# Attention and a low-rank mixer on one core: q, k and v loaded into 112 partitions in place of 128

## The chip, the core and the metric

The kernel runs on one core of a Trainium2 chip. The metric is the device time of one execution in microseconds (us), here the median of three runs. The five engines are TensorE (PE in the profile; PEld is its weight load), VectorE (DVE), ScalarE (ACT), GpSimd (POOL) and SyncE (SP), which only issues transfers. Sixteen DMA engines carry the transfers that SP, ACT and POOL issue.

## The reference

For each of 8 batches and 12 heads, with sequence S = 448 and head size D = 64, queries and keys are normalised by their root mean square and a gain, attention is a plain softmax, and the heads of a batch are laid side by side (768 columns). A low-rank mixing over the sequence (rank 32) is added, and a two-layer network with 3072 hidden columns follows, with a residual.

```
q_n, k_n = rmsnorm(q, g_q), rmsnorm(k, g_k)
attn = softmax(q_n @ k_n.T / sqrt(64))
x = heads side by side of (attn @ v)            # (8, 448, 768)
u = x + (x.T @ U @ V).T
out = u + relu(u @ w_ch1) @ w_ch2
```

All inputs and the output are float32.

## The kernel before, in words

A sequence of 448 rows is held as 112 partitions by NJ = 4 rows: partition p holds rows 4p to 4p+3 of a head, 4 x 64 floats, 1 KB that lie together in memory. SP = 112 is that number of partitions (a name in the code, not the engine), P = 128 is the whole of SBUF's partitions. Since a head is 112 such pieces and heads follow each other, pieces 112 to 127 counted from a head's start are the first sixteen pieces of the next head.

The work on heads goes by groups t of four heads (24 groups; `load` and `load_v`, L199 and L204), and by pairs p of two heads (48 pairs, two to a group). `heads` (L188) builds the source pattern of a load: rows, heads, 256 floats. `load_pair` (L195) loads one pair's q or k, 128 or 112 rows of two heads; the first pair is loaded head by head, q by SP and k by ACT (L856 to L859). `load_v` loads v of a group, four heads in one transfer. Buffers lie in turns in three fixed places for q and k (`qkL`, and part of `hT`) and in a few places for v (`vt`, slots of `comb`, part of `hT`); the profile names the transfers by these places.

What is done with a pair: `squares` (L218) on ACT or POOL, `reduce` (L232) on DVE, `rsqrt` (L236) on ACT, `scale` (L241) on DVE or, from pair 12, POOL; then a transposition on PE (pairs 0 to 11) or by a DMA transpose from SP (`dma_transposes`, L277), the scores (L296), the exponentials on ACT (L304), the products with v (L311) and the normalisation on DVE (L326, L335). `cast_v` (L213) on POOL turns v to bf16. All of these read rows 0 to 111 of what was loaded.

The order is written by hand. The first batch follows a list of words, HEAD (L720): `sq`, `R`, `q`, `S` are the four steps above, `T`/`Tq`/`Tk`/`Tl` transposes, `Eq`/`Ek`/`El` their copies out of PSUM, `SC` and `X` scores and exponentials, `V` and `N` products and normalisation, `F` filler matmuls on PE, `G` and `GC` the gains and their copy on ACT, `cast` v's cast, `w` a load of weights by POOL, `late` small preparations on POOL, `MT`/`t`/`MU`/`u` the mixing, `B` the first matmuls of the network. Each engine takes its instructions in this order. ISSUE (L853) hangs the loads of groups 3 and 4 onto three of the words. All loads of groups 0 to 2, U and V stand ahead of it on SP (L856 to L868).

After the head, the network's steps (`mlp_first` L440, `mlp_single` L471, `mlp_pair` L522) fill PE, and the attention and mixing of the later batches are woven between them by weights (`weave`, L686). Loads of group t+3 and v of group t+2 are issued in `attention` (L658 to L662), groups 6 and 7 after a `touch` (L208, one memset on DVE, so that the loads have one thing to wait for). The weights w1 and w2 are loaded by POOL (L177, L181) with a cast to bf16, in six transfers each.

Before the change, `heads` gives 128 rows unless the load reaches the last head of the last batch, where 128 rows would run past the input: there it gives 112. Those are the second pair's q and k of group 23, and its v.

Of the kernel before, what the change touches and what calls it, by code (L numbers as in the profile page):

```python
# [18 lines left out]
def kernel(  # L19
# [14 lines left out]
    B, H, S, D = q.shape  # L34
# [5 lines left out]
    P = 128  # L40
    NJ = 4
    SP = S // NJ
# [144 lines left out]

    def heads(x, h, n):  # L188

        rows = P if h + n < B * H else SP  # L190
        src = x.rearrange("b h s d -> (b h) s d")[h:h + n].rearrange("h (p j) d -> p h (j d)", j=NJ)
        (ps, _), (hs, _), (ls, ln) = src.ap
        return rows, bass.AP(src.tensor, src.offset, [[ps, rows], [hs, n], [ls, ln]])

    def load_pair(eng, t, s, a, hs=slice(0, 2)):  # L195
        rows, src = heads((q, k)[s], HG * t + 2 * a + hs.start, hs.stop - hs.start)
        eng.dma_start(qk_of[t][0:rows, a, s, hs], src)
# [6 lines left out]
    def load_v(t):  # L204
        rows, src = heads(v, HG * t, HG)
        nc.sync.dma_start(v_of[t][0:rows], src)
# [746 lines left out]
```

## Time and profile before

| | us |
|---|---|
| median of 3 runs (566.09 to 568.92) | 568.36 |
| the profiled execution | 566.27 |
| its span, first to last instruction | 564.5 |
| TensorE busy / VectorE / ScalarE / GpSimd | 552.0 / 339.7 / 303.8 / 179.3 |

The core moved 72.39 MB in 108284 packets, 56.78 MB of it read from memory. The page gives, for each engine, the busy time, its share of the span and the number of instructions; then the span in 40 equal slices (14.1 us each) with the busy share of each in tenths; then the chain of work that ended last, by engine. The order of work gives start and duration of an instruction, and in brackets the idle time of its engine just ahead of it with what ended that. A line on transfers gives destination and source, the issuing queue, the number, the size of one, and the median time from issue to landing.

### The profile page before, as it was taken

The page shows a single profiled execution, that of the slowest core. Times are in us where ns is not written, and L with a number is a line of the kernel's source. Part 1 is how long each engine was busy: PE and PEld are TensorE (multiplying, and loading weights), DVE is VectorE, ACT ScalarE, POOL GpSimd, SP SyncE. Part 2 cuts the span into 40 slices and gives each one's busy share as a digit, 9 for nine tenths or more (in the row PEclk, how much of TensorE's full clock was granted, in tenths as well). Part 3 has the DMA queues.
Part 4 walks back from the last instruction along what each step waited for, and adds up shares of the span by engine and source line. Part 5 has one row for each costly group of instructions (what it writes and reads, how often), then busy time and mean ns, then how long its engine had stood idle before and what let it go on. Part 6 is the DMA issues. An engine that isn't in the chain of part 4 may idle for free.

```text
span 564.5 us, 13202 instructions
## 1 busy us (share of the span) xinstructions
PE 552.0 (98%) x5469; PEld 388.2 (69%) x5469; DVE 339.7 (60%) x766; ACT 303.8 (54%) x515; POOL 179.3 (32%) x175
## 2 busy tenths in 40 slices
PE   7999999999999999999999999999999999999996
PEld 3665665767768677576785785776867768677774
DVE  5967858487665655656665577465565644643332
ACT  7966640779347663488448781765716745112020
POOL 5966016444051340432404430434104320010202
PEclk9999999999999999999999999999999999999999
DMA  8999996946455561365357563634615101030102
GB/s 275 283 243 239 204 253 174 206 130 168 129 96 150 144 155 48 76 187 142 87 143 160 130 176 85 152 94 143 168 29 125 30 17 59 15 99 1 57 1 57
DMA packets 108284, 72.39 MB, mean 128 GB/s; under 512 B 56656, under 2 KB 104768, under 8 KB 108224
## 3 DMA queue, kind: packets, MB, share of 16 engines
q1 hardware_dynamic: 96704, 61.70, 41.9%
q0 software_dynamic: 11008, 9.44, 10.3%
q8 instruction: 43, 0.70, 0.5%
q10 hardware_dynamic: 512, 0.41, 0.2%
q14 instruction: 17, 0.14, 0.1%
HBM read 56.78 MB, written 11.01 MB: 120 GB/s over the span
## 4 chain that ended last, share of the span: by engine, by line
PE 89%; ACT 4%; DVE 2%; DMA 2%; issue 1%; SPq 0%; POOLq 0%
PE ph L529 32%; PE po L512 29%; PE o L311 7%; PE po L467 5%; PE sc L296 4%; PE ph L449 3%; PE sh L296 3%; ACT E L304 2%; PE px L388 1%; ACT hT L421 1%; DMA hT<-in_moe_V_dram 1%; DMA qk<-in_q_dram 1%; PE bank L311 1%; PE sc L710 1%; PE ph L477 1%
## 5 line engine op out<-in xcount | busy, mean ns | idle before, releaser
L529 PE MATMUL ph<-ur,w1b 128*128 128x256 bf16 x1728 | 202.7, 273 | 0.0
L529 PEld LDWEIGHTS <-w1b 128*128 128x128 bf16 x1728 | 164.0, 98 | 29.1 <-issue 9.1
L512 PEld LDWEIGHTS <-hT 128*128 128x128 bf16 x1032 | 96.5, 98 | 65.0 <-issue 7.9
L421 ACT ACTIVATE hT<-ph 128x512 bf16<-128x512 f32 (+1 forms) x112 | 65.5, 587 | 116.1 <-PE ph L529 108.6
L304 ACT ACTIVATE E<-sc 112x896 bf16<-112x896 f32 x138 | 123.1, 918 | 2.3 <-PE sc L296 2.3
L248 POOL TENSOR_TENSOR qkn<-qk,rms 112x512 bf16<-112x512 f32 x72 | 80.4, 1138 | 111.2 <-ACT rms L239 86.5
L512 PE MATMUL po<-w2b,hT 128*128 128x384 bf16 (+1 forms) x588 | 103.6, 323 | 0.2 <-ACT hT L421 0.2
L304 ACT ACTIVATE E<-sh 112x448 bf16<-112x448 f32 x108 | 52.9, 543 | 78.6 <-PE sh L296 78.6
L520 DVE TENSOR_TENSOR hT<-hT 128x512 bf16<-128x512 bf16 x144 | 68.4, 492 | 21.3 <-ACT hT L421 19.0
L512 PE MATMUL po<-comb,hT 128*128 128x384 bf16 (+1 forms) x444 | 78.3, 322 | 0.0
L569 POOL TENSOR_TENSOR osb<-osb,xr 128x384 f32<-128x384 f32 x12 | 12.9, 1072 | 189.1 <-DVE osb L568 168.1
L423 DVE TENSOR_SCALAR hT<-ph 128x512 bf16<-128x512 f32 (+1 forms) x58 | 38.7, 667 | 55.6 <-PE ph L529 52.7
L311 PEld LDWEIGHTS <-E 112*128 112x128 bf16 x1536 | 61.1, 98 | 9.0 <-issue 1.9
L311 PE MATMUL o<-va,E 112*128 112x65 bf16 x1344 | 57.0, 194 | 0.2
L326 DVE RECIPROCAL rec<-o 128x4 f32<-128x4 f32 x84 | 15.1, 180 | 50.1 <-PE o L311 50.0
L296 PE MATMUL sc<-qkT 64*128 64x448 bf16 x268 | 39.7, 351 | 1.8 <-ACT E L304 1.1
L233 DVE TENSOR_REDUCE sums<-sq 112x16 f32<-112x1024 f32 x32 | 38.7, 1209 | 3.9 <-ACT sq L228 3.8
L467 PE MATMUL po<-w2b,hT 128*128 128x384 bf16 x192 | 34.7, 326 | 0.1
L228 ACT ACTIVATE sq<-qk 112x1024 f32<-112x1024 f32 x32 | 33.8, 1057 | 0.0
L335 DVE TENSOR_TENSOR xr<-o,rec 128x192 bf16<-128x192 f32 (+1 forms) x108 | 31.6, 311 | 2.9
L581 POOL TENSOR_TENSOR osb<-osb,part 128x768 f32<-128x768 f32 x12 | 21.8, 1814 | 35.7 <-DVE part L579 35.7
L390 DVE TENSOR_TENSOR xr<-px,xr 128x384 bf16<-128x384 f32 x56 | 29.5, 550 | 5.9 <-PE px L386 3.2
(120 smaller groups left out, 444.3 us busy)
## 6 DMA issues: line engine op xcount, KB each, us to landing
qk<-in_q_dram SPq DMA_DIRECT2D x44, 256.0 KB, 4.2
qk<-in_k_dram SPq DMA_DIRECT2D x44, 256.0 KB, 4.7
vt<-in_v_dram SPq DMA_DIRECT2D x17, 512.0 KB, 5.8
w1b<-in_moe_w_ch_dram POOLq DMA_DIRECT2D x6, 768.0 KB, 21.0
w2b<-in_moe_w_ch_dram POOLq DMA_DIRECT2D x6, 768.0 KB, 34.2
out_dram<-osb SPq DMA_DIRECT2D x8, 336.0 KB, 3.0
comb<-in_v_dram SPq DMA_DIRECT2D x5, 512.0 KB, 9.0
out_dram<-osb SPq DMA_DIRECT2D x7, 288.0 KB, 2.9
```

Of the source, the lines that this page charges most:

```text
L228: nc.scalar.activation(dst, src, AF.Square)
L233: nc.vector.tensor_reduce(rs_of(p, of=sums).rearrange("p (s h j) -> p s h j", s=2, h=2)[:, :, hs], sqs[p].rearrange("p (s h j d) -> p s h ...
L248: (nc.gpsimd if p >= 12 else nc.vector).tensor_tensor(out[:, g], x[:, g], rs[:, g].to_broadcast([SP, g.stop - g.start, NJ, D]), OP.mult)
L296: nc.tensor.matmul(sc[hh][0:n, 0:S], flat[pp, c:c + n], blocks(p)[pp, :, 0], start=True, stop=True)
L304: nc.scalar.activation(dst, src, AF.Exp, scale=float(D) ** 0.5)
L311: nc.tensor.matmul(o[:, i, :], E[:, hh, c:c + P], va[:, hl, kc, :], start=(kc == 0), stop=(kc == NJ - 1))
L421: nc.scalar.activation(out, ph, AF.Relu)
L423: nc.vector.tensor_relu(out, ph)
L467: nc.tensor.matmul(po, left(hc), w2b[:, half, hc, :], start=(hc == 0), stop=(hc == KH - 1))
L512: nc.tensor.matmul(bank, left[:, k, :], right[:, k, cols], start=start and k == 0, stop=k == KH // 2 - 1, skip_group_check=not start)
L520: pending.append(lambda: fn(*args))
L529: nc.tensor.matmul(out, w1b[:, dc, hc * P:(hc + 1) * P], u[:, dc, :], start=(dc == 0), stop=(dc == KD - 1))
```

## The change

`heads` takes 112 rows always, not only at the end of the input. Nothing else differs: the same transfers are issued at the same places, each with 112 pieces of 1 KB for each head in place of 128.

```diff
     def heads(x, h, n):

-        rows = P if h + n < B * H else SP
+        rows = SP
         src = x.rearrange("b h s d -> (b h) s d")[h:h + n].rearrange("h (p j) d -> p h (j d)", j=NJ)
         (ps, _), (hs, _), (ls, ln) = src.ap
         return rows, bass.AP(src.tensor, src.offset, [[ps, rows], [hs, n], [ls, ln]])
```

## The prediction

> **What bounds the kernel now.** I read the page from the top, then its chain, then the waits and the order of work in the first 36 us, and last the transfers with their times to landing.
>
> ```profile
> span 564.5 us, 13202 instructions
> PE 552.0 (98%) x5469; PEld 388.2 (69%) x5469; DVE 339.7 (60%) x766; ACT 303.8 (54%) x515; POOL 179.3 (32%) x175
> PE   7999999999999999999999999999999999999996
> PEclk9999999999999999999999999999999999999999
> DMA  8999996946455561365357563634615101030102
> PE 89%; ACT 4%; DVE 2%; DMA 2%; issue 1%; SPq 0%; POOLq 0%
> ```
>
> TensorE is busy 552.0 of 564.5 us, at a granted clock that stays at its top, and 89% of the chain is its own work. The loads that the change touches are 2% of the chain at most. The DMA row is full only at the start. So the change can act in two ways: in the first slice of PE (a 7), which waits for the first loads, and through weights that share the 16 DMA engines with the loads until about 86 us.
>
> The windows of the first 15 us show what PE loses there: 3.68, 3.08 and 4.40 us busy of 5.00 each, so 3.8 us idle, 1.3 of it ahead of the first matmul; part of the busy time is warm-up. The order of work shows what the loads have to do with it (start, duration, then the idle time ahead and who ended it):
>
> ```profile
> 6.91 1.06 ACT L228 ACTIVATE comb<-qk 112x1024 f32<-112x1024 f32 x1 [0.68 <-DMA qk<-in_k_dram]
> ...
> 8.00 1.22 DVE L233 TENSOR_REDUCE sums<-comb 112x16 f32<-112x1024 f32 x1 [0.99 <-ACT gcol L838]
> 8.06 0.81 PE L700 MATMUL sc<-xr 128*128 128x512 bf16 x3 [1.07 <-ACT gcol L838]
> ...
> 8.53 1.06 ACT L228 ACTIVATE w2b<-qk 112x1024 f32<-112x1024 f32 x1 [0.52 <-DMA qk<-in_k_dram]
> ...
> 9.95 1.90 POOL L230 TENSOR_TENSOR w2b<-qk 112x1024 f32<-112x1024 f32 x1 [2.43 <-DMA qk<-in_k_dram]
> ```
>
> Pair 1's squares (6.91) wait for their k. The copy GC is queued behind them on ACT (7.87); the reduction R1 (8.00) and PE's fillers (8.06) wait for GC. From 8.00 on DVE is full: the windows give it 4.96, 4.93, 4.90 and 4.90 us of 5.00 from 10 to 30 us, and from 25 us PE is full too. So R1's start passes through to the end, by DVE first and by PE's queue after. That is the change's one lever on the path.
>
> **The change part by part.** (1) Bytes. Section 6 of the page lists 49 loads of q, 49 of k and 24 of v, 122 in all; three (two of 224 KB, one of 448 KB) have 112 rows already. The other 119 shrink by an eighth: 92 of 256 KB by 32, four of 128 KB by 16, 23 of 512 KB by 64, which is 4480 KB: 4.59 of 72.39 MB, and 4480 of 108284 packets, each of them 1 KB. No instruction, issue or wait is added or removed: every reader reads rows 0 to 111 only, and rows past them are read by nobody.
>
> (2) Issue. SP spent 0.42 and 0.45 us on the two 112-row loads at 399.67 and 400.14 us, and 0.42 to 0.47 on 128-row ones beside them. Cost nothing; no queue is passed.
>
> (3) Time of one transfer. The trace has three of the new form, and neighbours of the old:
>
> ```profile
> vt<-in_v_dram SPq DMA_DIRECT2D x1, 512.0 KB, 6.1
> qk<-in_q_dram SPq DMA_DIRECT2D x1, 256.0 KB, 3.2
> qk<-in_k_dram SPq DMA_DIRECT2D x1, 256.0 KB, 3.6
> qk<-in_q_dram SPq DMA_DIRECT2D x1, 224.0 KB, 5.4
> qk<-in_k_dram SPq DMA_DIRECT2D x1, 224.0 KB, 5.4
> ```
>
> These are the five loads of the last group at 398.5 us, issue to landing. In fifteen earlier groups the third and fourth load, with 128 rows, took 3.3 to 5.4 and 3.5 to 6.7 us, medians 4.2 and 4.8. So two of the new form, with an eighth fewer bytes, landed 1.2 and 0.6 us later than the median of the old. From landing to landing, second to fourth, that is 2.82 us against a median of 2.04 (1.23 to 4.78): 0.39 us more for each load. The lone v of 448 KB reads better:
>
> ```profile
> GB/s 389 307 184 102 102 189 191 205 174 90 41 118 268 260 135 145 61 48 96 273 307 369 389 389 355 273 143 61 27 0 0 0 0 0 0 0 0 0 0 0
> vt<-in_v_dram SPq DMA_DIRECT2D x1, 448.0 KB, 3.9
> ```
>
> This is the window 434 to 440 us in slices of 0.15 us: once it runs it moves 389 GB/s, the rate that 128-row loads reach (374 to 386 in the head at 2 to 3.4 us). From 3.2 us for a first 256 KB and 389 GB/s for the rest, 448 KB in the old form would take 3.7 and 512 KB 3.9 (an estimate). It took 3.9.
>
> So the bounds are: an eighth off each transfer's moving time, or 0.39 us more for each load. I take a value near nothing with a small gain, because the lone load is the one whose rate can be read without a neighbour, and the two late ones lie inside the old form's spread.
>
> [...]
>
> (4) The head. After the four 128 KB loads (the last lands at 4.12 us) two 256 KB loads land until 6.84 us, pair 1's k last: 2.72 us. An eighth of that is 0.34 us, and the gate cannot give more than ACT's 0.68 us of waiting. Behind it sq2 (8.53) and POOL's squares (9.95) wait for loads too; they would land up to 0.5 and 0.7 us earlier by the same share, so they follow and set no new gate. What is late next is POOL's own work ahead of ACT's squares (Sk0 and Sl0, 6.31 to 7.51). Forecast: 0 to 0.34 us less, taken as 0.2.
>
> (5) The weights. w1's six chunks land at 27.6, 33.9, 40.2, 46.4, 52.7 and 57.5 us (issue plus time to landing). PE runs hidden chunks of 128 columns in 1.53 us each (38.3 to 69.0 us, twenty of them), so from the second on they are needed at 38.3, 44.5, 50.6, 56.8 and 62.9: 4.1 us of cover at least. w2's first lands at 61.4, needed at 69.0. Earlier landings here buy nothing, since no PE wait of this stretch is put down to a transfer of weights; later ones cost only beyond 4.1 us.
>
> (6) The steady part. No ACT square after 9 us waits for a load. The tightest covers are pair 16 (k lands 106.3, squares at 107.46) and pair 38 (325.74, 326.65): 1.1 and 0.9 us. Earlier landings change nothing; landings 1.2 us later would cost 0.1 and 0.3 us on ACT.
>
> Sum: the profiled execution took 566.27 us, 1.77 around its span of 564.5. 566.27 - 0.2 = 566.1. That execution was 2.09 us below the median of the runs shown, 568.36; with the same step the forecast is 568.2.
>
> **Rivals.** (A) The forecast: a landing moves by under 0.35 us, the head by 0 to 0.34: 568.0 to 568.4. For it: the lone load's 389 GB/s and its unchanged 3.9 us. Against: the full DMA row at the start, where an eighth could count for more.
> (B) Bytes count in full, and the gate yields all of its 0.68 us: 567.7. For it: the landings of the head come one behind another, at 311 to 330 GB/s. Against: the first 256 KB loads land 0.9 us apart, though 16 engines at 389 GB/s would need 0.67, so bytes are not all of it.
> (C) Slower: 112 rows make each transfer 0.39 us longer. It decides as soon as the second 256 KB load is late: pair 1's k by 0.8 us, pair 3's (six loads on) by 2.3. POOL's squares then end at 14.2 in place of 11.85, and R3, now at 12.01, starts at 14.2: the head loses 2.2 us. The two tight places add 0.4 at most, and w1, with eight q and k loads and two v loads of twice the size beside it, would be late by 0.39 x 12 = 4.7 us, 0.6 beyond its cover. Together 0.8 to 3.2 us: 569.2 to 571.6, taken as 570.6. For it: 5.4 us twice. Against: the old form's spread.
> (D) The change doesn't reach the bytes (fewer engines take a load, or packets of another size). The three loads of that form moved in 1 KB packets, with completions from 16 engines, so I give it nothing of its own.
>
> **How the numbers follow.** A 0.62, B 0.14, C 0.24. The predicted time is A's, 568.2. Runs of before spread over 566.09 to 568.92, so a median can lie 1.4 us off by sampling alone: A and B reach down to 566.2, and leaving the top of C (beyond 571.0, with sampling) about 2 in 10 is left out. Range 566.0 to 571.0. Half a per cent, about what a measurement of this kernel can tell from no change, is 2.8 us: below 565.5 or above 571.2. A gives 0.03 on either side, B 0.10 below, C 0.45 above: faster 0.04, same 0.83, slower 0.13.
>
> **What would show it.** After the change: 103804 packets, 67.8 MB, 112-row loads only. (3) and (4): the idle time ahead of ACT's squares at 6.91 falls from 0.68 to between 0.3 and 0.6, and R1 starts at 7.7 to 8.0; B has it below 0.1, C above 1.2. (5): last w1 chunk within 1 us of 57.5, no PE wait at L449. (6): no DMA wait at L228 after 9 us. I am wrong if the time moves while the landings of the head don't, or if a 112-row load runs at clearly another rate beside the weights' transfers than alone: no row of before shows that mixture.

## The result and the profile after

The changed kernel takes 568.98 us (median of 22 runs, 567.64 to 572.64), the kernel before 567.85 us in the runs beside them (22 runs, 566.09 to 569.41). The ratio is 1.0021 with a 95% interval of 1.0011 to 1.0031: a loss of about 1.1 us. The forecast of 0.2 us less had the wrong sign, though the time lies inside the range.

Executions of every kernel here, before's too, differ in the mean granted clock of TensorE: runs of before at 0.998 or more (the high clock) take 566.5 us on average (51 runs in three batches: 566.55, 566.52, 566.34), those at 0.991 to 0.997 (the lower clock) 568.4 (54 runs: 568.47, 568.44, 568.23). Where less than 1 us matters, runs of like clock are compared. The profile of before has 0.999, that of the changed kernel (569.13 us) 0.994. From the page of the changed kernel, in its order:

```profile
span 567.4 us, 13201 instructions
...
PE   7998999999999999999999999999999999999996
...
PEclk8999999999999999999999999999999999999998
DMA  9999995956546542265256563534715101040101
...
DMA packets 103804, 67.80 MB, mean 120 GB/s; under 512 B 56656, under 2 KB 100288, under 8 KB 103744
...
PE 89%; ACT 5%; DVE 3%; issue 1%; DMA 1%; POOLq 0%; SPq 0%; DVEq 0%; ACTq 0%
```

PEclk begins and ends with an 8 where before had a 9, and so is the fourth digit of PE (42.6 to 56.7 us). In the chain DVE has 3% in place of 2 and transfers 1% in place of 2: in whole per cents, some of the path has gone over from loads to VectorE. The DMA row is as full at the start as before, with fewer bytes to move. The span is 2.9 us longer. First starts of three groups of matmuls tell where. These are two of the groups and PE's busy time from 50 to 60 us (durations in ns, then first and last start; the window's length, then PE's busy time), before and then after:

```profile
L710 PE MATMUL sc<-ur,w1b x24: 322/326/337, 32.0 to 38.0; 128*128 128x384 bf16 x24
...
L467 PE MATMUL po<-w2b,hT x192: 322/326/337, 68.9 to 123.3; 128*128 128x384 bf16 x192
...
50.00:60.00 10.00, 10.00 (x114) 6.28 (x113) 8.53 (x19) 5.30 (x9) 3.92 (x3) 1.00 1.24 220
```

```profile
L710 PE MATMUL sc<-ur,w1b x24: 322/326/337, 33.5 to 39.5; 128*128 128x384 bf16 x24
...
L467 PE MATMUL po<-w2b,hT x192: 323/326/337, 71.8 to 126.2; 128*128 128x384 bf16 x192
...
50.00:60.00 10.00, 8.71 (x87) 5.04 (x86) 9.29 (x15) 5.21 (x10) 4.97 (x4) 1.00 1.24 220
```

| us | before | after |
|---|---|---|
| first matmul of the network (L710) starts: end of the head | 32.0 | 33.5 |
| from there to the first at L467 (68.9, 71.8), the stretch shared with the weights | 36.9 | 38.3 |
| first to last start at L529, the rest | 422.0 | 422.0 |

**The stretch shared with the weights** loses 1.4 us, at full clock. All but 0.1 us of it is lost in one wait; the waits of PE between 50 and 60 us have no such line before:

```profile
PE ph L449 <- DVE xr L339: 1.3, 1, 1.3
```

The order of work on POOL and DVE around it (start, duration), before and then after:

```profile
47.77 1.91 POOL L230 TENSOR_TENSOR comb<-qk 112x1024 f32<-112x1024 f32 x1
51.77 1.90 POOL L230 TENSOR_TENSOR comb<-qk 112x1024 f32<-112x1024 f32 x1 [2.09 <-DMA qk<-in_k_dram]
...
49.84 1.22 DVE L248 TENSOR_TENSOR qkn<-qk,rms 112x1024 bf16<-112x1024 f32 x1
```

```profile
49.20 3.75 POOL L230 TENSOR_TENSOR comb<-qk 112x1024 f32<-112x1024 f32 x2
52.89 1.04 POOL L214 CAST va<-comb 112x1024 bf16<-112x1024 f32 x1
...
51.29 3.72 DVE L248 TENSOR_TENSOR qkn<-qk,rms 112x1024 bf16<-112x1024 f32 x1
```

Before, POOL made the squares of pair 10, waited 2.09 us for pair 11's k, and made those of pair 11. DVE's scaling of pair 8 (L248) fell into that wait and took 1.22 us. After, pair 11's k is there in time: POOL runs both squares and the cast of v without a break (49.20 to 53.93), and the same scaling takes 3.72 us, ending 1.08 us after the cast. The normalisation queued behind it on DVE (L326 to L339) is late, and PE waits for that. Nothing is lost by the load itself: it is lost because a wait on POOL is gone.

The k was there in time because it landed sooner after its issue: at 50.44 us in place of 51.61, though the later head had put its issue off by 1.4 us. This is the transfers view from 36 to 56 us, where chunks of w1 and w2 run beside group 5's loads (k and v; size, median time from issue to landing), of before and of after:

```profile
qk<-in_k_dram SPq DMA_DIRECT2D x2, 256.0 KB, 10.6
comb<-in_v_dram SPq DMA_DIRECT2D x1, 512.0 KB, 16.4
```

```profile
qk<-in_k_dram SPq DMA_DIRECT2D x2, 224.0 KB, 9.0
comb<-in_v_dram SPq DMA_DIRECT2D x1, 448.0 KB, 14.5
```

One by one, group 5's q, k, q, k and v took 6.4, 8.3, 10.0, 12.9 and 16.4 us before, and 6.0, 7.6, 8.9, 10.4 and 14.5 after. Beside the weights, an eighth fewer packets did land earlier, and in each execution profiled: pair 11's k took 10.4 to 10.5 us in all eight profiles of this document with 112 rows in group 5, and 11.4 to 13.1 in the six with 128.

**The head** did not get earlier loads. The transfers view from 8.5 to 14 us, in slices of 0.14 us, when the first v and most of groups 1 and 2 land, before and after:

```profile
GB/s 372 380 380 387 387 387 380 387 395 380 380 387 380 395 380 387 380 380 365 343 357 358 350 343 343 365 350 350 358 350 317 343 378 313 358 216 198 170 138 114
```

```profile
GB/s 276 268 231 268 268 231 223 209 223 238 276 298 216 171 186 231 268 291 216 216 268 223 238 283 298 238 253 268 231 268 283 283 223 276 238 238 292 287 248 253
```

The view has the engines full in every slice of both, but for the last two of before. Up to 13.3 us the rate was 313 to 395 GB/s before; after it is 171 to 298, while the bytes fell by an eighth. It is so in every profile of this document: from 5 to 10 us, eight heads loaded with 112 rows move 284 to 306 GB/s, six with 128 rows 337 to 364. Pair 3's k lands at 10.2 us in the middle of the eight (9.6 to 10.9), and at 9.6 in the six (9.3 to 10.1).

The head's 1.5 us in this profile can be the clock alone: it has half clock from 8.0 to 11.4 us, and the windows of 5 to 10 and 10 to 15 us give it 0.80 and 0.86, where before had 1.00. The profile of e1_only5 below has 128-row loads in the head and the same 0.80 and 0.86, and its head ends at 33.6 us.

### The profile page after: what moved, and what is told of

The parts are those of the page before. It is cut to its first block, busy times and chain, and to the rows that moved or that the text cites. A ratio compares the mean times of both kernels' runs of the same rounds, so it can differ in the third digit from the quotient of the medians.

```text
span 567.4 us, 13201 instructions
## 1 busy us (share of the span) xinstructions
PE 553.9 (98%) x5468; PEld 388.9 (69%) x5469; DVE 341.2 (60%) x766; ACT 303.8 (54%) x515; POOL 179.1 (32%) x175
## 2 busy tenths in 40 slices
DMA packets 103804, 67.80 MB, mean 120 GB/s; under 512 B 56656, under 2 KB 100288, under 8 KB 103744
## 4 chain that ended last, share of the span: by engine, by line
PE 89%; ACT 5%; DVE 3%; issue 1%; DMA 1%; POOLq 0%; SPq 0%; DVEq 0%; ACTq 0%
PE ph L529 32%; PE po L512 29%; PE o L311 7%; PE po L467 5%; PE sc L296 4%; PE ph L449 3%; PE sh L296 3%; ACT E L304 2%; PE px L388 1%; DVE qkn L248 1%; ACT hT L421 1%; PE bank L311 1%; DMA qk<-in_k_dram 1%; PE sc L710 1%; PE ph L477 1%
## 5 line engine op out<-in xcount | busy, mean ns | idle before, releaser
L529 PE MATMUL ph<-ur,w1b 128*128 128x256 bf16 x1728 | 202.7, 273 | 0.0
L529 PEld LDWEIGHTS <-w1b 128*128 128x128 bf16 x1728 | 164.0, 98 | 29.1 <-issue 9.1
L248 POOL TENSOR_TENSOR qkn<-qk,rms 112x512 bf16<-112x512 f32 x72 | 80.3, 1136 | 113.8 <-ACT rms L239 89.0
L423 DVE TENSOR_SCALAR hT<-ph 128x512 bf16<-128x512 f32 (+1 forms) x58 | 38.7, 667 | 56.1 <-PE ph L529 52.7
L326 DVE RECIPROCAL rec<-o 128x4 f32<-128x4 f32 x84 | 15.1, 179 | 50.5 <-PE o L311 50.4
L233 DVE TENSOR_REDUCE sums<-sq 112x16 f32<-112x1024 f32 x32 | 38.7, 1210 | 3.9 <-ACT sq L228 3.8
L467 PE MATMUL po<-w2b,hT 128*128 128x384 bf16 x192 | 34.7, 326 | 0.1
L335 DVE TENSOR_TENSOR xr<-o,rec 128x192 bf16<-128x192 f32 (+1 forms) x108 | 31.6, 311 | 2.9
```

The lines of the kernel that those rows point to most:

```text
L233: nc.vector.tensor_reduce(rs_of(p, of=sums).rearrange("p (s h j) -> p s h j", s=2, h=2)[:, :, hs], sqs[p].rearrange("p (s h j d) -> p s h ...
L248: (nc.gpsimd if p >= 12 else nc.vector).tensor_tensor(out[:, g], x[:, g], rs[:, g].to_broadcast([SP, g.stop - g.start, NJ, D]), OP.mult)
L423: nc.vector.tensor_relu(out, ph)
L467: nc.tensor.matmul(po, left(hc), w2b[:, half, hc, :], start=(hc == 0), stop=(hc == KH - 1))
L529: nc.tensor.matmul(out, w1b[:, dc, hc * P:(hc + 1) * P], u[:, dc, :], start=(dc == 0), stop=(dc == KD - 1))
```

## The experiments

Two theories were open at first. The collision: group 5's earlier landing puts POOL's squares and cast in front of DVE's scaling. The rival: it is all in the head, by the clock or by the loads there. The expectations call the collision theory 1, the clock theory 2, slower 112-row loads theory 3, and, from e10_head on, slower 112-row loads in the head alone theory 4. Each kernel was timed in five rounds beside the kernel before; a ratio is to before, with its 95% interval. The view of the window from 50 to 60 us gives PE's busy time of 10, and L248 the scaling of pair 8.

**e1_only5**: before, with 112 rows in group 5's q and k alone.

```diff
-        rows = P if h + n < B * H else SP
+        rows = SP if h + n == B * H or (x is not v and h // HG == 5) else P
```

> The kernel before with one part of the change alone: only the four q and k loads of group 5 have 112 rows. Theory 1 (POOL's squares of pairs 10 and 11 run without a gap since group 5 lands earlier, and VectorE's scaling of pair 8 is held up by them: 3.72 us in place of 1.22): 0.7 to 1.3 us slower than before, the scaling at about 50 us over 2.5 us long, TensorE idle by about 1.3 us between 50 and 60 us. Theory 2 (the first 25 us lose the time, by TensorE's clock at half between 8.0 and 11.4 us): no difference from before. Theory 3 (112-row transfers are slower as such): no difference, or squares of pair 11 that wait longer than 2.1 us.

568.26 against 567.46 us, ratio 1.0016 (0.9997 to 1.0036), not told apart from before. The scaling took 2.36 us, PE stayed full (10.00). POOL still waited 1.52 us for pair 11, whose squares began at 50.81 and held the scaling (51.42) until they ended. Pair 11's k took 10.5 us, as after the whole change; but POOL came to pair 10's squares at 47.40, in place of 49.20 after, and so it still had to wait. What the other loads have to do with that is not shown. The one profile is of the lower clock; the 7 runs at the high clock take 567.84 us, 1.4 above before's 566.5 (0.5 to 2.2), so group 5's loads alone seem to cost something in other executions.

**e2_not5**: the changed kernel with 128 rows in group 5's q and k alone.

```diff
-        rows = SP
+        rows = P if x is not v and h // HG == 5 else SP
```

> The changed kernel with the four q and k loads of group 5 back at 128 rows. Theory 1: the scaling of pair 8 takes about 1.2 us again, TensorE is full between 50 and 60 us, and the time is 0 to 0.3 us below before. Theory 2: as slow as the changed kernel, 1.0 to 1.4 us above before. Theory 3: 0.9 to 1.3 us above before.

567.57 us, ratio 1.0007 (0.9992 to 1.0021). The scaling is back at 1.21 us, PE at 10.00. Group 5's loads are needed for the collision.

**e3_wait8**: the changed kernel, all rows 112, with POOL held: it copies one element of the scaled pair 8 before the squares of pair 11 and the cast, which are moved behind it.

```diff
...
-                add(0, scale, p + 1)
+                add(0, scale, p + 1); [add(0, *x) for x in ((marks, 8), (squares, 11), (cast_v, 4)) if p == 7]
...
-                    if p != 8:
+                    if p != 8 and (p, a) != (6, 1):
...
-            if not odd and t + 1 < NT:
+            if not odd and t + 1 < NT and p != 6:
...
+    marks = lambda p: nc.gpsimd.tensor_copy(mark, qkns[p][0:1, 0, 0, 0:1])
```

> The changed kernel, all loads at 112 rows, but POOL waits for VectorE's scaling of pair 8 (a copy of one element) ahead of the squares of pair 11. Theory 1: the scaling takes 1.2 us, TensorE loses nothing between 50 and 60 us, time 0 to 0.3 us below before. Theory 2 and 3: as slow as the changed kernel, 1.0 to 1.4 us above before.

567.91 us, ratio 1.0006 (0.9992 to 1.002). The scaling took 1.71 us, PE 10.00. But the added item shifts other woven pieces, so e9_wait_clean was made to repeat it without that.

**e4_heat**: the changed kernel with three more filler matmuls, spread so that TensorE has work through the head.

```diff
-        sq00:a sq01:a R00 q00 R01 q01 rk00 rk01 sq1:a Sq01 Sk0 G GC Sl0 Sq00 Tk0:0 F3:w Tl0:1
+        sq00:a sq01:a R00 q00 R01 q01 rk00 rk01 sq1:a Sq01 Sk0 G GC Sl0 Sq00 F3:1 Tk0:0 F3:1 Tl0:1
```

> The changed kernel with TensorE's filler matmuls of the first 8 us in a bank of their own, so that they don't wait for the gains' copy, and three more of them. Theory 2: the clock stays at its top from 5 to 15 us and the time falls by about 1.2 us, to that of before. Theory 1: the scaling of pair 8 still takes over 2.5 us and most of the loss of 1.2 us stays; at most 0.5 us goes. Theory 3: the loss stays.

568.43 us, ratio 1.0023 (1.0004 to 1.0043). In its profile the clock is 1.00 from 5 to 15 us and PE is busy 5.00 of 5.00 from 5 to 10, yet the scaling takes 4.08 us and PE is busy 8.36 of 10. A head at full clock does not remove the loss: the clock alone is not its cause. (Its four runs at the lower clock take 570.7 us, 2.3 above before's; why is open.)

**e5_rest**: 112 rows everywhere but in groups 3 to 5. **e6_mid**: 112 rows in groups 3 to 5 alone (and in the last group's three loads, as before).

```diff
-        rows = P if h + n < B * H else SP
+        rows = P if h + n < B * H and 3 <= h // HG <= 5 else SP
```

```diff
-        rows = P if h + n < B * H else SP
+        rows = P if h + n < B * H and not 3 <= h // HG <= 5 else SP
```

> The change in all groups but 3, 4 and 5, whose q, k and v keep 128 rows: the head's loads and all late ones have 112. Theory 1 (VectorE's scaling of pair 8 is held up by POOL, which no longer waits for group 5): as before, 0 to 0.3 us below it, scaling 1.2 us long, no idle TensorE from 50 to 60 us. Theory 2 (the head loses it): all of the loss, 1.0 to 1.4 us above before. Runs are to be compared among those of like mean clock too: the runs of before fall into two, about 566.5 us with a mean clock of 0.998 or 0.999 and about 568.4 us with one below; by theory 1 both stay where they are.

> The change in groups 3, 4 and 5 alone (q, k and v), all others as before. Theory 1: all of the loss, 1.0 to 2.0 us above before, in the runs of high mean clock too; scaling of pair 8 over 2.5 us long, TensorE idle by 0.7 to 1.6 us between 50 and 60 us. Theory 2: no difference from before.

Before took 567.74 us beside these two. e5_rest: 567.35 us, 1.0007 (0.9986 to 1.0028), scaling 1.22 us. e6_mid: 568.43 us, 1.0024 (1.0011 to 1.0036), with the clock at 1.0 in the profile and the head's loads as before. Its order of work, and its waits of PE from 50 to 60 us:

```profile
48.21 3.75 POOL L230 TENSOR_TENSOR comb<-qk 112x1024 f32<-112x1024 f32 x2
51.90 1.04 POOL L214 CAST va<-comb 112x1024 bf16<-112x1024 f32 x1
...
50.36 3.67 DVE L248 TENSOR_TENSOR qkn<-qk,rms 112x1024 bf16<-112x1024 f32 x1
```

```profile
PE ph L449 <- DVE xr L339: 1.2, 1, 1.2
```

It is the same picture as after the whole change, POOL without a break and the scaling ending 1.09 us after the cast. Three groups of 24 give as much loss as the whole change. The other 21 give none that can be told from before, though that interval is too wide to exclude it; at the high clock e5_rest takes 566.89 us (7 runs) and e6_mid 568.75 (6). A loss with an undisturbed head, by the same wait, decides for the collision as the larger part.

**e7_block**: before, no load changed, with POOL's squares of pair 10 made twice, so that POOL is busy when the scaling comes.

```diff
-                        add(0, squares, (10 if p == 6 else 12) + a)
+                        add(0, lambda n: [squares(n) for _ in range(2 if n == 10 else 1)], (10 if p == 6 else 12) + a)
```

> The kernel before, no load changed, but POOL makes the squares of pair 10 twice, 1.9 us of work that needs no load and ends before the squares of pair 11 could start by their load. Theory 1: the scaling of pair 8 is held up as after the change (3 to 3.7 us in place of 1.2), TensorE loses 0.7 to 1.3 us between 50 and 60 us, and the time rises by as much. Theory 2 and 3: no difference, since POOL was idle there by 2.1 us.

567.21 us, ratio 1.0004 (0.9987 to 1.002). Its order of work:

```profile
47.22 3.88 POOL L230 TENSOR_TENSOR comb<-qk 112x1024 f32<-112x1024 f32 x2
51.37 2.56 POOL L230 TENSOR_TENSOR comb<-qk 112x1024 f32<-112x1024 f32 x1 [0.27 <-DMA qk<-in_k_dram]
...
49.45 2.72 DVE L248 TENSOR_TENSOR qkn<-qk,rms 112x1024 bf16<-112x1024 f32 x1
```

The scaling grew from 1.22 to 2.72 us by POOL's work alone, and ends 1.07 us after the doubled squares (51.10). So POOL's work holds the scaling without any change of a load. The price was below what was expected: PE lost 0.29 us. The 0.27 us that POOL still waited for the load let DVE in.

**e9_wait_clean**: the changed kernel with POOL held behind the scaling of pair 8, as e3_wait8, and all other pieces kept in their places.

```diff
...
-                add(0, scale, p + 1)
+                add(0, scale if p != 7 else scale_first, p + 1)
...
-                        add(0, squares, (10 if p == 6 else 12) + a)
+                        add(0, squares if (p, a) != (6, 1) else id, (10 if p == 6 else 12) + a)
...
-                add(0, cast_v, t + 1)
+                add(0, cast_v if p != 6 else id, t + 1)
...
+    def scale_first(p):
+        scale(p)
+        nc.gpsimd.tensor_copy(mark, qkns[p][0:1, 0, 0, 0:1])
+        squares(p + 3)
+        cast_v(4)
```

> The changed kernel, all loads at 112 rows; POOL waits for VectorE's scaling of pair 8 ahead of the squares of pair 11 and the cast behind them, with every other piece at its old place. Theory 1: scaling 1.2 to 1.9 us, TensorE full from 50 to 60 us, 0 to 0.4 us below before; runs of high mean clock at 566.2 to 566.6. Theory 2 and 3: as slow as the changed kernel, 1.0 to 1.4 us above before.

567.18 us, ratio 1.0004 (0.999 to 1.0018). Its order of work:

```profile
48.73 1.91 POOL L230 TENSOR_TENSOR comb<-qk 112x1024 f32<-112x1024 f32 x1
51.99 0.18 POOL L716 COPY mark<-qkn 1x1 bf16<-1x1 bf16 x1 [1.34 <-DVE qkn L248]
52.13 1.88 POOL L230 TENSOR_TENSOR comb<-qk 112x1024 f32<-112x1024 f32 x1
...
50.71 1.22 DVE L248 TENSOR_TENSOR qkn<-qk,rms 112x1024 bf16<-112x1024 f32 x1
```

All loads have 112 rows and land early, POOL waits 1.34 us by the hold, the scaling takes 1.22 us, PE is full from 50 to 60 us. Giving the wait back takes away most of the loss.

**e10_head**: 112 rows in groups 0 to 2 alone.

```diff
-        rows = P if h + n < B * H else SP
+        rows = P if h + n < B * H and h // HG > 2 else SP
```

> The change in groups 0 to 2 alone, the loads of the first 16 us. In the profiles so far, loads of 112 rows in this stretch landed 0.75 to 0.9 us behind one another, those of 128 rows 0.65 to 0.7. Theory 4 (in the head, where loads alone fill the DMA engines, a 112-row load is the slower one): pair 1's k lands at 7.0 to 7.6 us in place of 6.5 to 7.4, pair 3's at 10.2 to 10.9 in place of 9.4 to 10.2, and the runs of high mean clock are 0.2 to 0.6 us above those of before. Theory 1 alone (only the squares of pair 11 matter): within 0.2 us of before. Neither expects a longer scaling of pair 8.

568.06 against 566.88 us, ratio 1.0011 (0.9996 to 1.0026). At the high clock it takes 567.24 us (4 runs) where before takes 566.5: four runs can't size it. The five kernels with a 112-row head and no loss at 50 us in their profiles (e2, e3, e5, e9, e10) have 26 runs of that clock, 566.89 us on average: 0.4 us above before's 566.47 (0.2 to 0.6). Their 34 runs at the lower clock take 568.36, before's 568.38: nothing. Of the profiles with full clock in the head, three with 112 rows there (e2, e4, e9) end it at 32.5 to 32.9 us, five with 128 rows at 31.6 to 32.6. So the loads of the head seem to cost about 0.4 us by themselves. This is not as well shown as the collision: the five kernels were put together afterwards, and only e3 and e9 hold POOL back, so that in runs of the others that were not profiled part of the 0.4 may be the collision.

**e11_both**: 128 rows in groups 0 to 2, 112 in all others, and POOL held as in e9_wait_clean: meant to take out both losses and keep the fewer bytes. **e8_wait_before**: before with the same hold and no load changed.

```diff
-        rows = P if h + n < B * H else SP
+        rows = P if h // HG < 3 else SP
```

> Groups 0 to 2 at 128 rows, groups 3 to 23 at 112, and POOL waits for the scaling of pair 8 ahead of the squares of pair 11. Theories 1 and 4 together: both losses are gone and what is left of the earlier landings in the stretch of the weights is kept: 0 to 0.4 us below before, runs of high mean clock at 566.1 to 566.6. If either theory is wrong it is 0.3 us or more above before.

> The kernel before, 128 rows, with the same wait on POOL. Theory 1: no gain over before, since there POOL leaves the gap by waiting for the load: within 0.3 us of before in runs of like mean clock. If the wait helped by something else (a cast moved, for one), it would be faster here too.

e11_both: 567.87 us, ratio 1.0003 (0.9988 to 1.0019); at the high clock 566.59 us (5 runs). e8_wait_before: 568.05 us, 1.0012 (0.9995 to 1.0029); at the high clock 566.51 (3 runs; its median is high because 9 of its 12 runs had the lower clock). With both taken out, 4.0 MB fewer bytes (4480 KB less 3 x 192) bring nothing that these runs can show, and neither does the hold cost anything that they show.

**e12_after**: the changed kernel once more.

> The changed kernel once more, beside the others on their chip. Theories 1 and 4: 1.0 to 2.2 us above before, also in runs of high mean clock; scaling of pair 8 over 2.5 us long; pair 1's k at 6.6 to 7.9 us. Theory 2 (TensorE's clock alone): runs of like mean clock as before.

568.39 us, ratio 1.0020 (1.0004 to 1.0037), the same loss again. Its profile, however, shows the scaling at 2.39 us, below the 2.5 expected, and PE full from 50 to 60 us: here POOL waited 0.63 us for pair 11's load. The collision does not come in each execution at its full price.

**The price in one table.** Eight profiles, ordered by the scaling's duration:

| | POOL's wait ahead of pair 11's squares | scaling | ends after POOL's instruction | PE idle, 50 to 60 us |
|---|---|---|---|---|
| before | 2.09 (load) | 1.22 | not held | 0.00 |
| e9_wait_clean | 1.34 (hold) | 1.22 | not held | 0.00 |
| e1_only5 | 1.52 (load) | 2.36 | 1.08 (squares, 52.70) | 0.00 |
| e12_after | 0.63 (load) | 2.39 | 1.08 (squares, 53.15) | 0.00 |
| e7_block | 0.27 (load) | 2.72 | 1.07 (squares, 51.10) | 0.29 |
| e6_mid | none | 3.67 | 1.09 (cast, 52.94) | 1.24 |
| after | none | 3.72 | 1.08 (cast, 53.93) | 1.29 |
| e4_heat | none | 4.08 | 1.09 (cast, 53.40) | 1.64 |

The idle time is the scaling's duration less 2.43 us, within 0.01, in all of the last four: DVE had 1.2 us of cover there, and what goes beyond passes through to PE one for one. From L710 to L467 these four take 37.3, 38.2, 38.3 and 38.7 us, before 36.9, and the nine other profiles 36.4 to 37.0.

## Why the prediction was wrong, point by point

(1) Bytes: right, 103804 packets and 67.80 MB. (2) Issue: right, a median of 0.45 us for each load after, 0.46 before.

(3) Time of one transfer: no single value exists, and the one taken came from the wrong company. I took the lone load, 389 GB/s, which was its peak in two slices of the view. Where loads alone fill the engines (from pair 1's q to pair 3's k, landing to landing), a 112-row one takes 0.78 us in the middle for 224 KB, a 128-row one 0.69 for 256 KB. The first v takes 1.8 us in the middle (448 KB, 1.6 to 2.0) against 1.5 (512 KB, all six heads with 128 rows). So about 0.1 us more for a q or k and 0.3 for a v, where the bound of 0.39 had been read off five loads issued together. Beside the weights the sign turns: pair 11's k falls from 12.9 to 10.4. The runs gave a loss for each transfer in the head and a gain beside the weights, where one value had been taken for both.

(4) The head: forecast 0 to 0.34 us less, measured about 0.4 more at the high clock (e10_head, with its limits). The gate that I watched behaved as forecast in the profile after: the idle time ahead of the squares (now 6.70) is 0.51 and R1 starts at 7.79. But its pair 1's k, at 6.61 us, is the earliest of the eight heads with 112 rows (7.2 in the middle, up to 7.84), against 6.8 in the middle of six with 128 (6.45 to 7.35). So the agreement in that one profile was luck, and the later landings (pair 3's k, the first v at 12.0 against 11.2) are later in the middle, not earlier.

(5) The weights: the failing step. "Earlier landings here buy nothing" put them at 0, with who waits for the transfers of weights as the only reason. That held: w1's last chunk lands at 57.8 us. But I did not ask who profits from POOL's waiting for a load, though before's POOL waits 2.71, 2.91 and 2.09 us for k loads in this stretch. What the runs showed in place of the 0 is up to 1.6 us of PE idle (1.29 in the profile after), and it appeared as the wait at L449 that the prediction had named as not to come. No rival had this mechanism either; the text closest to it is its last sentence, that no row of before shows a 112-row load beside the weights.

(6) The steady part: right. ACT's squares wait for no load after 9 us, and the last part takes 422.0 us in both.

Rival C had the sign in the head, at about 0.4 us and not 0.8 to 3.2. The medians' 1.1 us are then the collision, 0 to 1.6 us by execution, and the head, about 0.4 at the high clock. How they share it is not settled: e6_mid loses 2.3 us against before among runs at the high clock (568.75, 6 runs), more than the 1.24 of its profile, and nothing among those at the lower clock (568.24 against 568.38). The changed kernel loses 1.9 (568.41, 9 runs of two batches; 1.3 to 2.6) and 0.6 (25 runs; 0.1 to 1.0). Why the loss is larger at the high clock is open.

Two more points stay open. Why a 112-row load is slower where loads alone fill the engines (0.78 us against 0.69) was not tried. And whether 112-row heads make the low clock more frequent: 63 of 106 runs against 86 of 165 with 128-row heads, which chance alone can give.

## What to carry to other kernels

Before counting an earlier load as harmless, look at who waits for it and which other engine works in that wait: a gap on one engine can be another's slot (here 2.09 us of waiting on POOL, in which DVE's scaling took 1.22 us and not 3.72), and closing it moves work that nobody ordered. Price a transfer by neighbours in the same company (alone, behind others of its kind, beside another queue), since the same change gave both signs in one kernel (0.69 to 0.78 us in the head, 12.9 to 10.4 beside the weights). Where the order between two engines matters, write it down as a wait; no cost of it could be seen here (e8_wait_before: 566.51 us at the high clock, before 566.5).

## What the runs showed of the hardware

VectorE's scaling of pair 8, 1.22 us where nothing held it, did not run beside GpSimd's squares (1.9 us) or cast (1.04 us) here. It ended 1.07 to 1.10 us after the GpSimd instruction that held it in all eight profiles where it was held (the six of the table, e3_wait8 and e11_both), whatever its start. The other way round, squares that began while the scaling ran took 2.43 to 2.59 us in place of 1.9 (e2_not5, e5_rest, e7_block, e10_head). VectorE lost again at the next instruction in the three profiles where POOL had no break (after, e4_heat, e6_mid): the scaling began before the second squares had ended and was held through the cast as well, 3.67 to 4.08 us in all. Why it got in between squares and cast in e1_only5 and e12_after (2.36 and 2.39 us) is open, and what keeps the two engines apart was not shown.

TensorE's granted clock fell to half within the first 15 us in some profiles and stayed at 1.00 in others, before's among them. In the profile after it was half for 3.41 us (7.95 to 11.37). In e10_head (0.82 from 5 to 10 us, 0.84 from 10 to 15) and e12_after (0.92 and 0.73) the same two windows add up to 3.4 and 3.5 us at half. e12_after is the changed kernel too, and there the dip fell later; why was not shown. Heads with the dip end at 33.5 to 34.0 us, heads without at 31.6 to 32.9. The runs of before with a lower mean clock are 1.9 us of 567 longer (566.5 against 568.4). A difference of 0.2% between a few runs is best read among runs of like clock.
